# Keys of two batches and queries of the last rows turned by transposing transfers instead of TensorE, with a new order of work: a 4-batch attention and MLP kernel on one core

## Chip, cores and metric

One core of a Trainium2 chip runs the whole kernel. The time is device microseconds (us) of one execution. The kernel before took 652.37 us (median of 3 runs, 651.45 to 653.49).

## What is computed

Attention of 4 batches and 8 heads over 576 rows of 64 elements, with a bias that a small network makes from the distance of two rows, and then an MLP over the 2304 x 512 result:

```python
scores = scale * np.matmul(q, k.transpose(0, 1, 3, 2))
rel = (pos[:, None] - pos[None, :]).astype(np.float32)
psi_i = np.log1p(np.maximum(pos[:, None].astype(np.float32), 1.0))
x = (np.log1p(np.abs(rel)) / psi_i)[..., None]
bias = np.maximum(x @ w1 + b1, 0.0) @ w2          # hidden 32, one value per head
attn = softmax(scores + bias.transpose(2, 0, 1)[None])
h = attn_out @ w_in                               # 512 -> 2048
out = (h * (1.0 / (1.0 + np.exp(-1.702 * h)))) @ w_out
```

The weights come as 64-bit floats and are put together on VectorE.

## The kernel before

Every matmul that matters is made of fp16 halves: a value is scaled and rounded to fp16 (`hi`, on ScalarE or VectorE), and what is left over is rounded again (`lo`, always VectorE, helper `lo_part` at L735). A product takes three matmuls (hi hi, hi lo, lo hi).

The batches go in two pairs, (0, 1) and (2, 3). A pair has five chunks of query rows, c = 0 to 3 with 128 rows and c = 4 with the last 64. A *unit* is one batch, one chunk and one pair of heads (two pairs of heads for c = 4): 36 units a pair, 72 in all. A unit runs: scores on TensorE (L899) into the PSUM tile `sp`; bias added and row minimum taken on VectorE (L908); the exponential on ScalarE (L917); hi (L938 on ScalarE or L934 on VectorE) and lo (L735) of the weights into a `wide` tile; that tile turned so that the keys lie on partitions, and the matmuls with v (L1004). The first 8 units are turned on TensorE (L953, L958, copied out at L963 or L965) and multiplied at L980. The other 64 are turned by one transposing transfer each, issued by SP (L989), 18 blocks of 128 x 128 fp16. The halves of the result (`xT`) feed the MLP: L1211 (w_in), tanh and gate (L1219 to L1240), L1249 (w_out), eviction (L1255) and the store (L1265). The bias is made on TensorE from relu tiles (L621 on ScalarE, L623 on VectorE; products at L640), evicted (L643), stored to a scratch in DRAM (L659) and loaded per unit pair (L719).

Keys: per batch and half of the heads one tile (`load_k`, L797; e = 0, 1), 8 tiles in all. The key rows 512 to 575 of a pair of batches come apart (`load_kt`, L789). `trans_k` (L810) turns a tile on TensorE into `sp`: 8 fp32 transposes (L815) and two small matmuls for the last 64 keys (L816). ScalarE evicts the hi half (L830), VectorE the lo half (L835, shown as L735, 128 x 1152 from PSUM).

Queries: c = 1 to 3 of all batches and c = 0 of batches 2 and 3 are split in their own layout (L761, L763) and turned by a transposing transfer of 8 blocks on SP's queue (L766), 14 of them. The others, c = 0 of batches 0 and 1 and c = 4 of all four batches, are turned on TensorE (`trans_q`, L752 to L756).

The order is made while the program is built. Each piece of work is a task for one engine with its inputs, its estimated cost, the buffers it takes and gives back, and a priority. `Plan.order` (L58) plays the tasks through and, whenever an engine is free, gives it the ready task with the lowest number, if its buffers are free. The numbers come from the list `TURNS` (L230), one per task in the order in which the tasks are made; the strings `WHERE` (L220) say for each task that could run on either which engine it gets (A ScalarE, V VectorE, P GpSimd). The result is one fixed instruction order per engine and per DMA queue. All loads, all transposing transfers and all stores to the scratch are issued by SP, in one row. There are 18 `wide` buffers (128 x 1152 fp32) and 8 `narrow` ones (128 x 576); `LEAST` (L428) keeps at least so many of a kind free for each use.

A task with a `gate` starts only behind the scores of an earlier unit; for a key load that was 2 units before its first use (`K_FROM`, L446).

Of the kernel before, what the change touches and what calls it, by code (L numbers as in the profile page):

```python
# [1355 lines left out]
```

## Time and profile before

| what | value |
|---|---|
| median of 3 runs | 652.37 us (651.45 to 653.49) |
| the profiled execution | 654.06 us |
| its span | 652.3 us, 22886 instructions |
| TensorE matmul / weight load busy | 608.8 us (93%) / 432.6 us (66%) |
| VectorE / ScalarE / GpSimd busy | 509.2 (78%) / 398.6 (61%) / 74.6 us (11%) |
| transfers of SP's queue (q1) | 104.81 MB, 74.4% of the DMA engines' time |
| chain that ended last, by engine | PE 74%, DVE 14%, ACT 5%, issue 3%, DMA 2% |

A busy share is an average over stages; what bounds a stage is read from that stage's rows. TensorE's matmuls overlap, so its busy time stands for "had work", and idle time before an instruction says what it waited for. The span lies 1.8 us under the profiled execution's own time, and that execution 1.7 us over the median.

### The profile page before, as it was taken

To read this page: it belongs to the slowest core of one execution; us is meant where nothing else is said; L and a number is where in the kernel's file an instruction comes from. 1 tells how busy PE (TensorE), PEld (TensorE's weight loads), DVE (VectorE), ACT (ScalarE), POOL (GpSimd) and SP (SyncE) were. 2 spreads that over 40 slices of the span, in tenths; PEclk is the share of its full clock that TensorE was granted. 3 is DMA by queue.
4 is the path that set the end of the run, shared out by engine and by line. 5 is a ranking of instruction groups with operands and counts; after the bars stand their busy time and mean duration, and the time that the engine had idled before them with its cause. 6 is when DMAs were issued, how large, how long until landed. Compare 5 with 4: busy or idle time off the path is not lost.

```text
span 652.3 us, 22886 instructions
## 1 busy us (share of the span) xinstructions
PE 608.8 (93%) x9712; PEld 432.6 (66%) x9712; DVE 509.2 (78%) x1371; ACT 398.6 (61%) x870; POOL 74.6 (11%) x116
## 2 busy tenths in 40 slices
PE   5579877998899999999999999999999999999997
PEld 3236555675576667657677667677777777878775
DVE  7989997999997967783869999996895898423232
ACT  6988854988788745662657577665753655322222
POOL 3000000111110110011200010101112011001211
PEclk9969995999999999999999999999999999999999
DMA  9987863899969985989899999998986897500000
GB/s 273 310 285 229 219 215 111 170 236 232 214 232 205 166 164 121 193 173 216 199 202 197 191 188 212 218 173 134 208 196 110 150 158 124 95 34 4 2 35 18
DMA packets 227542, 111.08 MB, mean 170 GB/s; under 512 B 207088, under 2 KB 211824, under 8 KB 227440
## 3 DMA queue, kind: packets, MB, share of 16 engines
q1 hardware_dynamic: 224672, 104.81, 74.4%
q10 hardware_dynamic: 2768, 4.81, 2.2%
q8 instruction: 76, 1.25, 0.8%
q14 instruction: 26, 0.21, 0.1%
HBM read 52.85 MB, written 15.34 MB: 105 GB/s over the span
## 4 chain that ended last, share of the span: by engine, by line
PE 74%; DVE 14%; ACT 5%; issue 3%; DMA 2%; SPq 1%; ACTq 0%; DVEq 0%
PE hp L1211 26%; PE op L1249 25%; PE sp L899 8%; PE hp L1004 7%; PE sp L640 3%; DVE wide L908 3%; DVE wide L735 2%; PE op L640 2%; PE op L958 2%; ACT wide L621 2%; DVE w L735 1%; DVE narrow L1141 1%; DVE narrow L1145 1%; PE hp L980 1%; DMA scr<-narrow 1%
## 5 line engine op out<-in xcount | busy, mean ns | idle before, releaser
L1211 PE MATMUL hp<-xT,w 128*64 128x256 f16 (+1 forms) x3840 | 207.1, 262 | 1.6 <-DVE w L735 1.0
L1249 PE MATMUL op<-w,gT 128*64 128x512 f16 x1728 | 204.5, 380 | 3.5 <-ACT gT L1233 1.5
L1211 PEld LDWEIGHTS <-w 128*64 128x64 f16 x3840 | 189.6, 110 | 19.6 <-issue 7.7
L1249 PEld LDWEIGHTS <-gT 128*64 128x64 f16 x1728 | 96.4, 110 | 78.8 <-issue 6.7
L917 ACT ACTIVATE wide<-wide,sm 128x576 f32<-128x576 f32 x144 | 110.9, 770 | 47.9 <-DVE sm L908 43.1
L1240 POOL TENSOR_TENSOR gT<-th,gT 128x256 f16<-128x256 f32 (+1 forms) x95 | 69.6, 734 | 570.9 <-ACT gT L1233 336.1
L1219 ACT ACTIVATE th<-hp 128x256 f32<-128x256 f32 (+1 forms) x160 | 57.1, 357 | 117.0 <-PE hp L1211 88.3
L1225 DVE SCALAR_TENSOR_TENSOR th<-th,hp 128x256 f32<-128x256 f32 (+1 forms) x160 | 62.4, 391 | 77.6 <-ACT th L1219 76.3
L908 DVE CUSTOM_DVE_ANT_0 wide<-sp,wide 128x576 f32<-128x576 f32 x144 | 105.8, 751 | 6.9 <-PE sp L899 2.7
L735 DVE SCALAR_TENSOR_TENSOR wide<-wide,sm,wide 128x576 f16<-128x576 f32 x128 | 104.4, 826 | 6.6 <-ACT wide L938 6.2
L899 PE MATMUL sp<-wide,narrow 64*128 64x512 f16 (+1 forms) x960 | 67.1, 289 | 12.5 <-DVE sm L908 7.2
L938 ACT ACTIVATE wide<-wide,sm 128x576 f16<-128x576 f32 x83 | 62.4, 767 | 7.8 <-DVE sm L926 2.0
L1004 PEld LDWEIGHTS <-v 128*64 128x64 f16 x2160 | 57.9, 111 | 5.7 <-issue 2.6
L1004 PE MATMUL hp<-wide,v 128*64 128x128 f16 (+1 forms) x2160 | 60.5, 214 | 0.4 <-DMA wide<-wide 0.4
L899 PEld LDWEIGHTS <-narrow 64*128 64x128 f16 (+1 forms) x960 | 28.9, 98 | 46.5 <-issue 28.3
L621 ACT ACTIVATE wide<-tab,bp 128x576 f32<-128x576 f32 x81 | 59.2, 772 | 0.2 <-PE sp L640 0.2
L1233 ACT CAST gT<-th 128x256 f16<-128x256 f32 (+1 forms) x84 | 32.0, 380 | 27.8 <-DVE th L1225 17.0
L640 PE MATMUL op<-wide,pk 128*32 128x512 f32 (+1 forms) x208 | 23.3, 518 | 10.0 <-ACT narrow L643 3.5
L623 DVE TENSOR_SCALAR wide<-tab,bp 128x576 f32<-128x576 f32 x63 | 31.3, 527 | 0.0
L1240 DVE TENSOR_TENSOR gT<-th,gT 128x256 f16<-128x256 f32 (+1 forms) x65 | 25.3, 390 | 6.0 <-ACT gT L1233 5.2
L640 PE MATMUL sp<-wide,pk 128*32 128x512 f32 (+1 forms) x368 | 28.4, 443 | 1.0 <-DVE sm L908 0.9
L1235 DVE CAST gT<-th 128x256 f16<-128x256 f32 (+1 forms) x76 | 21.3, 280 | 9.4 <-PE op L1249 7.3
(72 smaller groups left out, 494.3 us busy)
## 6 DMA issues: line engine op xcount, KB each, us to landing
wide<-scr SPq DMA_DIRECT2D x32, 576.0 KB, 5.1
scr<-narrow SPq DMA_DIRECT2D x31, 288.0 KB, 3.7
wide<-in_moe_w_in_dram SPq DMA_DIRECT2D x16, 512.0 KB, 5.4
wide<-in_moe_w_out_dram SPq DMA_DIRECT2D x16, 512.0 KB, 4.8
wide<-in_k_dram SPq DMA_DIRECT2D x16, 256.0 KB, 5.1
narrow<-in_q_dram SPq DMA_DIRECT2D x16, 256.0 KB, 4.4
out_dram<-narrow ACTq DMA_DIRECT2D x16, 256.0 KB, 3.1
wide<-scr SPq DMA_DIRECT2D x8, 288.0 KB, 5.0
```

Source lines behind the costliest of these rows:

```text
L621: nc.scalar.activation(out=h, in_=tv, func=ACTF.Relu, bias=bp[:, pb:pb + 1])
L640: nc.tensor.matmul(to[32 * r:32 * r + 32], lhsT=w2b, rhs=rhs, start=True, stop=True)
L735: nc.vector.scalar_tensor_tensor(out=out, in0=in0, scalar=scale, in1=in1, op0=ALU.mult, op1=ALU.subtract)
L899: nc.tensor.matmul(pair[64 * e:64 * e + m, a, cs], lhsT=qt[r, x, hp + e, 0:m], rhs=kt[r, hp % 2 + e, y, cs], start=i == 0, stop=i == 2,)
L908: nc.vector.tensor_tensor_reduce(out=slot(("a32", u))[:, cs], in0=slot(("sp", u)).rearrange("p (h a) n -> p h (a n)", h=2)[:, a, 0:S], in1 ...
L917: nc.scalar.activation(out=t, in_=t, func=ACTF.Exp, scale=-1.0, bias=sm[:, a:a + 1], accum_out=sm[:, 2 + a:3 + a])
L938: nc.scalar.activation(out=hl_of(u)[:, 0, cs], in_=slot(("a32", u))[:, cs], func=ACTF.Identity, scale=r)
L1004: nc.tensor.matmul(o[64 * a:64 * a + 64, po], lhsT=vt[:, x, vc:vc + 64], rhs=t[:, 9 * y + k0, po], start=kb < 0 and i == 0, stop=kb == 3 a ...
L1211: nc.tensor.matmul(p[y0:y0 + FF, :n], lhsT=wi16[:, f // 4, cc, z, w0:w0 + FF], rhs=r, start=i == 0, stop=i == 11, skip_group_check=FF < 128,)
L1225: nc.vector.scalar_tensor_tensor(out=th, in0=th, scalar=1.0, in1=slot(("hp", j, f))[:, :n], op0=ALU.add, op1=ALU.mult)
L1240: (nc.vector if on("low", NF * j + f) == "V" else nc.gpsimd).tensor_tensor(out=gt[:, 1, :n], in0=th, in1=gt[:, 0, :n], op=ALU.subtract)
L1249: nc.tensor.matmul(o[y0:y0 + FF, i], lhsT=gt[:, z, 128 * i + y0:128 * i + y0 + FF], rhs=wo16[:, NF - 1 - f, y, :], start=f == 0 and n3 == ...
```

## The change

Four things change.

1. **Keys of batches 2 and 3.** The four key tiles are no longer turned on TensorE. They are split in their own layout (`k_split`: hi on ScalarE for batch 2 and VectorE for batch 3, lo on VectorE, 128 x 1024), and one transfer per tile turns both halves (`turn_k`, 16 blocks). The last 64 keys of both batches are split and turned once (`kt_split`, `turn_kt`, 8 blocks), into a `narrow` buffer that is held until the pair's last scores and for which `LEAST` now keeps one. The loads may start 9 units before the first use instead of 2.
2. **Queries of c = 4.** The two batches of a pair share one tile: two loads, one split, one transfer of 8 blocks. Four tasks on TensorE become two transfers.
3. **The last store.** The second of the last two stores is issued by SP instead of ScalarE.
4. **Order and engines.** All numbers in `TURNS` are new, and the strings too. Counts of tasks on (ScalarE, VectorE), before to after: relu (81, 63) to (86, 58); exp, the hi half of the weights, (95, 49) to (77, 67), of which units 42 to 59 hold 14; turn, the copies of the first 8 units, (16, 8) to (22, 2); x (26, 46) to (30, 42); gate hi (84, 76) to (76, 84); weight hi (22, 10) to (21, 11). Gate lo (GpSimd, VectorE) goes from (95, 65) to (102, 58).

```diff
+        'khi': 'AAAAAAVV',
...
-        'turn': 'AAAAVAVVAAAAVAAAVVAVAVAA',
+        'turn': 'AAAAAAAAAAAAVAAAAAVAAAAA',
...
-             "narrow": {"w": 1, "os": 2, "qT": 2, "q": 1, "kt": 1, "ob": 1, "dg": 1, "qs": 1}}
+             "narrow": {"w": 1, "os": 2, "qT": 2, "q": 1, "kt": 1, "ob": 1, "dg": 1, "qs": 1, "kTt": 1}}
...
-    TURNED_Q = {(b, c) for b in range(B) for c in range(4) if b > 1 or c > 0}
+    TURNED_Q = {(b, c) for b in range(B) for c in range(5) if b > 1 or c > 0}
+    TURNED_K, KT_FROM = {1}, 9
...
+    def q_key(b, c):
+        return (b, c) if c < 4 else (b // 2 * 2, c)
...
-        t = slot(("q32", b, c))[:n, 0:512].rearrange("p (h d) -> p h d", h=H)
-        nc.sync.dma_start(out=t, in_=q[b, :, 128 * c:128 * c + n, :].rearrange("h p d -> p h d"))
+        for i in range(1 if c < 4 else 2):
+            t = slot(("q32", b, c))[n * i:n * i + n, 0:512].rearrange("p (h d) -> p h d", h=H)
+            nc.sync.dma_start(out=t, in_=q[b + i, :, 128 * c:128 * c + n, :].rearrange("h p d -> p h d"))
...
+    def k_split(b, e, z):
+        t, d = slot(("k32", b, e))[:, 0:1024], slot(("ks", b, e)).bitcast(F16)
+        if z:
+            lo_part(d[:, 1024:2048], t, KS, d[:, 0:1024])
+        elif on("khi", 2 * b + e) == "A":
+            nc.scalar.activation(out=d[:, 0:1024], in_=t, func=ACTF.Copy, scale=KS)
+        else:
+            nc.vector.tensor_scalar(out=d[:, 0:1024], in0=t, scalar1=KS, scalar2=None, op0=ALU.mult)
+
+    def turn_k(b, e):
+        nc.sync.dma_start_transpose(
+            out=slot(("kT", b, e)).bitcast(F16)[:, 0:2048].rearrange("p (c n) -> p c n", c=16),
+            in_=slot(("ks", b, e)).bitcast(F16)[:, 0:2048],
+        )
...
+    def turn_kt(g):
+        nc.sync.dma_start_transpose(
+            out=slot(("kTt", g)).bitcast(F16)[:, 0:1024].rearrange("p (c n) -> p c n", c=8),
+            in_=slot(("kts", g)).bitcast(F16)[:, 0:1024],
+        )
+
+    def k_of(b, hp, y, cs):
+        if b // 2 not in TURNED_K:
+            return k_out(b, hp // 2)[:, hp % 2, y, cs]
+        if cs.start == 0:
+            return slot(("kT", b, hp // 2)).bitcast(F16)[:, 0:2048].rearrange("p (x u n) -> p x u n", x=2, u=2)[:, y, hp % 2]
+        t = slot(("kTt", b // 2)).bitcast(F16)[:, 0:1024].rearrange("p (x u n) -> p x u n", x=2, u=NP)
+        return t[:, y, hp, ST * (b % 2):ST * (b % 2) + ST]
+
+    def add_turned_k(b, e):
+        p, g = due(first["k", b, e]) - K_LEAD, b // 2
+        if g not in kt_task:
+            ld = add("SP", 700, lambda: load_kt(g), take=[("narrow", "kt", ("kt", g))],
+                     gate=first["k", b, e] - KT_FROM, prio=p - LOAD_LEAD, dma=1200, n_dma=2, hold=4000)
...
+            kt_task[g] = add("SP", 1300, lambda: turn_kt(g), [lo], take=[("narrow", "kTt", ("kTt", g))],
+                             give=[("kts", g)], prio=p, dma=1350, hold=2000)
+        ld = add("SP", 700, lambda: load_k(b, e), take=[("wide", "kv", ("k32", b, e))],
+                 gate=first["k", b, e] - KT_FROM, prio=p - LOAD_LEAD, dma=2300, n_dma=2, hold=4500)
+        hi = either("khi", 2 * b + e, lambda: k_split(b, e, 0), {"A": act(1024), "V": dve(1024, fast=True)}, [ld],
+                    take=[("wide", "ks", ("ks", b, e))], prio=p)
+        lo = add("DVE", dve(1024), lambda: k_split(b, e, 1), [hi], give=[("k32", b, e)], prio=p)
+        kT_task[b, e] = add("SP", 2400, lambda: turn_k(b, e), [lo, kt_task[g]], take=[("wide", "kT", ("kT", b, e))],
+                            give=[("ks", b, e)], prio=p, dma=2700, hold=2000)
...
-                nc.scalar.dma_start(out=out[t:t + hi - lo, :], in_=ob[lo - 128 * i:hi - 128 * i, :])
+                q_ = nc.sync if j == len(blocks) - 1 and off else nc.scalar
+                q_.dma_start(out=out[t:t + hi - lo, :], in_=ob[lo - 128 * i:hi - 128 * i, :])
```

Two places of the new order. TensorE, before, where the first key tile of batch 2 is turned (`wide_86` is the key tile, `narrow_102` the last 64 keys, `idn` the identity), between the MLP's matmuls:

```order
L1211 LDWEIGHTS w_63
L1211 MATMUL hp_123<-xT_114,w_63 64x256
L815 MATMUL sp<-idn,wide_86 128x128 x4
L816 MATMUL sp<-idn,narrow_102 128x64
L815 MATMUL sp<-idn,wide_86 128x128 x4
L816 MATMUL sp<-idn,narrow_102 128x64
L1249 LDWEIGHTS gT_119
L1249 MATMUL op<-w_63,gT_119 64x512
```

After, the same keys appear on TensorE only in the scores (L957 there), `wide_93` being the turned tile and `narrow_108` the turned last keys:

```order
L957 MATMUL sp<-wide_93,narrow_104 128x512
L957 LDWEIGHTS narrow_104
L957 MATMUL sp<-narrow_108,narrow_104 128x64
L957 LDWEIGHTS narrow_104
L957 MATMUL sp<-narrow_108,narrow_104 128x64
L957 LDWEIGHTS narrow_104
L957 MATMUL sp<-wide_93,narrow_104 128x512
```

The transposes and the small matmuls are gone from TensorE's row, for all four tiles; the scores keep their shapes.

SP's queue, before, around the key loads of the second pair (L989 an attention turn, L766 a query turn, L719 a bias load, L799 and L792 key loads; the L989 here is the 25th):

```order
L743 DMA narrow_105<-in_q_dram 128x8x64
L989 DMA_TRANSPOSE wide_88<-wide_94 128x18x128
L719 DMA wide_100<-scr_79 128x1152
L799 DMA wide_86<-in_k_dram 128x8x64 x2
L792 DMA narrow_102<-in_k_dram 64x8x64 x2
L766 DMA_TRANSPOSE narrow_105<-narrow_104 128x8x128
L799 DMA wide_91<-in_k_dram 128x8x64 x2
```

After, from the 22nd attention turn (L1047 there) to the 25th; L848 turns the last keys, L835 a key tile, L803 loads one, L723 a bias load, L770 a query turn:

```order
L1047 DMA_TRANSPOSE wide_100<-wide_88 128x18x128
L835 DMA_TRANSPOSE wide_93<-wide_89 128x16x128
L663 DMA scr_83<-narrow_106 128x576
L663 DMA scr_83<-narrow_107 128x576
L1047 DMA_TRANSPOSE wide_85<-wide_90 128x18x128
L1047 DMA_TRANSPOSE wide_91<-wide_96 128x18x128
L723 DMA wide_87<-scr_83 64x1152 x2
L723 DMA wide_99<-scr_83 64x1152 x2
L723 DMA wide_97<-scr_79 128x1152
L803 DMA wide_94<-in_k_dram 128x8x64 x2
L835 DMA_TRANSPOSE wide_88<-wide_101 128x16x128
L770 DMA_TRANSPOSE narrow_104<-narrow_102 128x8x128
```

The key loads moved ahead by several attention turns, and the key turns stand behind the 22nd, 24th, 25th and 27th attention turn, with the turn of the last keys ahead of the 22nd.

## Rows read from the trace of the kernel before

**Rows 1.** Stretches: us, busy us (x count) of PE, PEld, DVE, ACT, POOL; TensorE clock; DMA share; GB/s

```profile
0.00:120.00 120.00, 89.55 (x854) 56.02 (x854) 106.06 (x248) 88.18 (x166) 4.97 (x21) 0.89 0.76 229
120.00:180.00 60.00, 55.40 (x880) 37.14 (x878) 59.59 (x133) 50.15 (x103) 10.38 (x12) 1.00 1.01 223
...
220.00:335.00 115.00, 115.00 (x1836) 80.47 (x1834) 83.99 (x239) 64.68 (x142) 15.08 (x19) 1.00 0.88 180
335.00:450.00 115.00, 112.65 (x2100) 82.26 (x2096) 104.32 (x316) 74.69 (x180) 11.65 (x18) 1.00 1.02 192
450.00:565.00 115.00, 115.00 (x1978) 84.81 (x1974) 94.42 (x267) 65.24 (x151) 16.80 (x21) 1.00 0.83 152
565.00:652.00 87.00, 81.22 (x1486) 65.74 (x1482) 25.35 (x76) 21.46 (x61) 11.71 (x20) 1.00 0.08 20
sum 652.00, PE 608.82 PEld 432.62 DVE 509.25 ACT 398.56 POOL 74.62; mean PE 86.97 PEld 61.80 DVE 72.75 ACT 56.94 POOL 10.66
```

**Rows 2.** Waits of PE, 185 to 652 us: us in total, times, longest us

```profile
PE sp L899 <- DVE wide L735: 1.5, 2, 1.2
...
PE hp L1004 <- DMA wide<-wide: 0.4, 1, 0.4
```

**Rows 3.** Timeline of PE at the first key tile: start us, us, line, instruction

```profile
331.11 0.66 PE L815 MATMUL sp<-idn,wide 128*128 128x128 f32 x4
...
332.48 2.78 PE L1249 MATMUL op<-w,gT 128*64 128x512 f16 x24
```

**Rows 4.** Timeline of PE at a query tail of 64 rows

```profile
528.95 0.46 PE L756 MATMUL sp<-idn,narrow 64*128 64x64 f32 x4
529.34 1.50 PE L1211 MATMUL hp<-xT,w 128*64 128x256 f16 x24
```

**Rows 5.** Timeline of ACT and its queue at the end

```profile
647.87 0.60 ACT L1255 ACTIVATE narrow<-op 128x512 f32<-128x512 f32 x1 [1.55 <-PE op L1249]
648.50 1.14 ACTq L1265 DMA_DIRECT2D out_dram<-narrow  x2
```

**Rows 6.** DMA, 545 to 575 us: queue with share; transfers with count, median us to landing

```profile
q1 hardware_dynamic: 9344, 2.36, 49.7%
...
wide<-wide SPq DMA_TRANSPOSE x4, 5.1
```

**Rows 7.** Timeline of SP's queue: attention turns 21 and 22, and 25

```profile
279.53 5.91 SPq L989 DMA_TRANSPOSE wide<-wide  x2
...
317.36 3.44 SPq L989 DMA_TRANSPOSE wide<-wide  x1
```

**Rows 8.** DMA, 335 to 450 us, same columns

```profile
q1 hardware_dynamic: 60495, 20.99, 98.7%
...
wide<-wide SPq DMA_TRANSPOSE x19, 6.9
```

**Rows 9.** Chain of waits at 339.55 us, then PE's timeline at 344.33 us

```profile
339.55 4.74 DMA wide<-wide
...
344.33 1.14 PE L1004 MATMUL hp<-wide,v 128*64 128x64 f16 x60 [0.43 <-DMA wide<-wide]
```

**Rows 10.** Groups by line and form: xcount, busy us, mean ns, idle before us

```profile
L735 DVE SCALAR_TENSOR_TENSOR wide<-sp,wide 128x1152 f16<-128x1152 f32 x8 | 10.8, 1352 | 2.0 <-ACT wide L830 2.0
...
L735 DVE SCALAR_TENSOR_TENSOR narrow<-narrow,narrow 128x512 f16<-128x512 f32 x14 | 9.6, 686 | 0.1
...
L934 DVE TENSOR_SCALAR wide<-wide,sm 128x576 f16<-128x576 f32 x45 | 24.5, 547 | 0.1
...
L965 DVE COPY wide<-op 128x512 f32<-128x512 f32 x7 | 4.8, 689 | 4.5 <-PE op L958 4.2 <-ACT wide L963 0.3
...
L623 DVE TENSOR_SCALAR wide<-tab,bp 128x576 f32<-128x576 f32 x63 | 31.3, 527 | 0.0
```

**Rows 11.** Timeline of PE: scores of units 42 and 60

```profile
379.80 0.91 PE L899 MATMUL sp<-wide,narrow 64*128 64x512 f16 x12
...
477.72 0.91 PE L899 MATMUL sp<-wide,narrow 64*128 64x512 f16 x12
```

More of the change, by code (lines that the diff above doesn't have):

```diff
@@ L530, in due @@
         return U_AT[0] + U_AT[1] * u if u < 8 else U_AT[2] + U_AT[3] * (u - 8)
+    def q_key(b, c):
+        return (b, c) if c < 4 else (b // 2 * 2, c)
     first = {}
     for u, (b, c, hp) in enumerate(units):
-        for key in (("q", b, c), ("k", b, hp // 2)):
+        for key in (("q",) + q_key(b, c), ("k", b, hp // 2)):
             first.setdefault(key, u)
@@ L741, in load_q @@
         n = q_n(c)
[L742 to L743 removed]
+        for i in range(1 if c < 4 else 2):
+            t = slot(("q32", b, c))[n * i:n * i + n, 0:512].rearrange("p (h d) -> p h d", h=H)
+            nc.sync.dma_start(out=t, in_=q[b + i, :, 128 * c:128 * c + n, :].rearrange("h p d -> p h d"))
     def q_out(b, c):
[L746 removed]
+        return slot(("qT",) + q_key(b, c)).bitcast(F16)[:, 0:1024].rearrange("p (x n) -> p x n", x=2)
     def q_psum(b, c):
         t = slot(("qp", b, c))
[L750 removed]
+        return (t[:, 0] if plan.env["qp", b, c][0] == "s" else t)[:, 0:512]
     def trans_q(b, c):
[L753 to L754 removed]
+        t, p = slot(("q32", b, c))[:, 0:512], q_psum(b, c)
         for hp in range(NP):
[L756 removed]
+            nc.tensor.transpose(p[:, 128 * hp:128 * hp + 128], t[:, 128 * hp:128 * hp + 128], idn)
     def q_split(b, c, z):
@@ L771, in add_q @@
     def add_q(b, c):
-        n, p = q_n(c), due(first["q", b, c]) - Q_LEAD
-        ld = add("SP", 350, lambda: load_q(b, c), take=[("narrow", "q", ("q32", b, c))],
-                 gate=first["q", b, c] - Q_FROM, prio=p - LOAD_LEAD, dma=9 * n, hold=4000)
+        n, p = 128, due(first["q", b, c]) - Q_LEAD
+        ld = add("SP", 350 if c < 4 else 700, lambda: load_q(b, c), take=[("narrow", "q", ("q32", b, c))],
+                 gate=first["q", b, c] - Q_FROM, prio=p - LOAD_LEAD, dma=9 * n, hold=4000, n_dma=1 if c < 4 else 2)
         if (b, c) in TURNED_Q:
@@ new lines, in kt_split @@
+    def kt_split(g, z):
+        t, d = slot(("kt", g))[:, 0:512], slot(("kts", g)).bitcast(F16)
+        if z:
+            lo_part(d[:, 512:1024], t, KS, d[:, 0:512])
+        else:
+            nc.scalar.activation(out=d[:, 0:512], in_=t, func=ACTF.Copy, scale=KS)
+    def turn_kt(g):
[10 more added lines that the diff above has]
+        return t[:, y, hp, ST * (b % 2):ST * (b % 2) + ST]
@@ new lines, in add_turned_k @@
+    def add_turned_k(b, e):
[3 more added lines that the diff above has]
+                     gate=first["k", b, e] - KT_FROM, prio=p - LOAD_LEAD, dma=1200, n_dma=2, hold=4000)
+            hi = add("ACT", act(512), lambda: kt_split(g, 0), [ld], take=[("narrow", "qs", ("kts", g))], prio=p)
+            lo = add("DVE", dve(512), lambda: kt_split(g, 1), [hi], give=[("kt", g)], prio=p)
+            kt_task[g] = add("SP", 1300, lambda: turn_kt(g), [lo], take=[("narrow", "kTt", ("kTt", g))],
[7 more added lines that the diff above has]
+                            give=[("ks", b, e)], prio=p, dma=2700, hold=2000)
@@ L821, in add_k @@
     def add_k(b, e):
+        if b // 2 in TURNED_K:
+            return add_turned_k(b, e)
         p = due(first["k", b, e]) - K_LEAD
@@ L889, in scores @@
         m, ne = (128, 1) if c < 4 else (64, 2)
-        n = q_n(c)
         qt = q_out(b, c).rearrange("p x (u n) -> p x u n", u=NP)
-        kt = k_out(b, hp // 2)
+        q0 = 0 if c < 4 else ST * (b % 2)
         pair = slot(("sp", u)).rearrange("p (h a) n -> p h (a n)", h=2)
@@ L899, in scores @@
                         nc.tensor.matmul(
-                            pair[64 * e:64 * e + m, a, cs], lhsT=qt[r, x, hp + e, 0:m], rhs=kt[r, hp % 2 + e, y, cs],
+                            pair[64 * e:64 * e + m, a, cs], lhsT=qt[r, x, hp + e, q0:q0 + m], rhs=k_of(b, hp + e, y, cs)[r],
                             start=i == 0, stop=i == 2,
@@ L1052 @@
             wb, wc, whp = units[w]
-            for kind, key, fn in (("k", (wb, whp // 2), add_k), ("q", (wb, wc), add_q), ("v", (wb, whp // 2), add_v)):
+            for kind, key, fn in (("k", (wb, whp // 2), add_k), ("q", q_key(wb, wc), add_q), ("v", (wb, whp // 2), add_v)):
                 if (kind, key) not in made:
@@ L1059 @@
         e2 = 1 if c < 4 else 2
-        st = s_task[u] = add("PE", 735, lambda u=u: scores(u), [qT_task[b, c], kT_task[b, hp // 2]],
+        st = s_task[u] = add("PE", 735, lambda u=u: scores(u), [qT_task[q_key(b, c)], kT_task[b, hp // 2]],
                              after=([s_task[u - 1]] if u else []) + [bias_pe[c]], mode=1,
@@ L1101 @@
             x_task[u] = add("DVE", 200, lambda u=u: x_split(u, 1), [go], give=[("ot", u)], prio=p - X_FIRST)
-            plan.extra(s_task[u], [("kT", b, hp // 2), ("qT", b, c)])
+            plan.extra(s_task[u], [("kT", b, hp // 2), ("qT",) + q_key(b, c)] + [("kTt", b // 2)] * (b // 2 in TURNED_K))
             continue
```

21 lines of the change are left out of this document (8 added, 13 removed), and 385 rows, old and new, of the table TURNS.

## The prediction

> **What bounds the kernel now.** I read the busy time by stretches first, because the whole-span shares mix two different regimes [rows 1]. In the first 180 us TensorE is idle for 30.5 us (120 less 89.55) and then 4.6 us (60 less 55.40), and its mean granted clock is 0.89 of full in the first 120 us: it waits for others. From 120 to 180 us VectorE is busy for 59.59 of 60 us, so that stretch is VectorE's, with the DMA at 1.01 beside it. From 220 us on the picture turns over. TensorE is busy in all of 220 to 335 us and all of 450 to 565 us, and in 112.65 of the 115 us between. At full clock, with no idle time, it sets the end: an instruction taken off it there moves everything behind it forward.
>
> The waits of TensorE behind 185 us say how near the other limits are [rows 2]. The largest is for VectorE, 1.5 us in all; a wait for a turned tile is there once, 0.4 us. So the order fits, but the stretch 335 to 450 us is tight three times over: TensorE full, VectorE 104.32 of 115 us, DMA share 1.02 [rows 1].
>
> **The change part by part.** *Keys off TensorE.* The first key tile of batch 2 starts at 331.11 us and the next work at 332.48 us: 1.37 us [rows 3]. All four tiles show this distance and lie between here and 373 us, so 4 x 1.37 = 5.5 us, where TensorE hardly waits. The scores keep their matmuls, so nothing comes back on TensorE.
>
> *Queries of 64 rows off TensorE.* One takes 529.34 less 528.95 = 0.39 us [rows 4], four of them 1.6 us, two at each pair's end, in the stretches without idle time. Again on the path.
>
> *Last store.* ScalarE ends the last eviction and issues two stores in 1.14 us [rows 5], 0.57 us each. With SP issuing the second at the same time, 0.55 us goes, bounds 0 and 0.6. Nothing else is queued on SP then; all its turns are long done.
>
> *DMA time added.* Where four attention turns run almost alone, the queue is busy for 49.7% of 30 us = 14.9 us, so 3.7 us for 18 blocks [rows 6], 0.21 us a block. A key turn (16 blocks) is then 3.3 us and a turn of 8 blocks 1.65 us. Four and three of them (last keys, two query tails): 18.2 us of DMA time, for 7.1 us of TensorE. The changed order puts two key turns, the last keys and one query tail near the 22nd to 24th attention turns, and two key turns behind the 25th and 27th. In the trace before, the 21st is issued at 279.53 us and the 25th at 317.36 us [rows 7]; the transfer of 339.55 us is the 27th by count. So 9.9 us falls ahead of about 335 us and 6.6 us behind; the second query tail comes near 530 us, where the DMA has 17% free [rows 1], and is hidden. From 220 to 335 us the DMA has 12% free, 14 us [rows 1]; from 335 to 450 us SP's queue alone takes 98.7%, which leaves 1.5 us, and a turn needs 6.9 us to landing against 5.1 us when alone [rows 8]. If half of the 14 us can be used (a turn can start only when its data is there), 16.5 less 7 = 9.5 us makes later turns late. How much of it reaches TensorE? Turn and matmul stand close: a turn issued at 339.55 us landed after 4.74 us and TensorE had waited 0.43 us for it [rows 9]. But the loads of keys now go ahead of the crowd, and MLP work is left over: behind 565 us TensorE still works for 81.22 us [rows 1], nearly all of it MLP. Bounds 0 and 16.5 us; I take 2 us, near the lower end, because a queue just as full cost TensorE only 0.4 us in all [rows 2].
>
> Which unit should turn is a point on which the Trainium skill has a rule, page "VectorE: DVE Perf Modes", section "Rules for kernel authors": a 128 x 128 transpose belongs on TensorE when PSUM may be its target, and on the DMA crossbar only otherwise; the section "The three transpose paths" has 390 ns against 1309 ns a block. By those figures the 88 blocks moved are an estimated 115 us of DMA, and the sum would be about 746 us if only the free 14 us hid any. The trace does not agree in size (0.21 us a block) and agrees in direction: more DMA time than TensorE time.
>
> *Splits.* VectorE loses four lo halves of 1152 from PSUM at 1352 ns [rows 10] and gains four of 1024 from SBUF. No row shows that form; 512 takes 686 ns [rows 10], so two of them, 1.37 us, are the upper end, and 1352 x 1024/1152 = 1.20 us the lower; I take 1.24. With two hi halves of 1024 (0.92 us each, from 527 ns for 576 columns [rows 10]) and one lo of 512 it is 7.5 against 5.4 us: 2.1 us more. ScalarE gets less of this work.
>
> *Engines re-dealt, second half.* Units 42 to 59 give 14 hi halves to VectorE, at 547 ns 7.7 us [rows 10]. These units run from 379.80 to 477.72 us [rows 11], where VectorE has 9.3% of 70 us and 17.9% of 28 us free [rows 1], 11.5 us, for the 9.8 us of both. If it fits, nothing; if VectorE is late, scores wait for its row minimum, as they do today. Bounds 0 and 9.8 us; I take 1 us, nearest the present 1.5 us of such waits.
>
> *Engines re-dealt, first 180 us.* VectorE loses five copies of 512 (689 ns) and one small one (some 0.3 us), and three relus at 527 ns [rows 10]: 5.3 us where it is full. ScalarE takes them; it was busy for 50.15 of 60 us, so it has room on average. Against it stands one `narrow` buffer of eight that is kept for the turned last keys from the start: bias evictions, weight merges and query tiles share those. No row prices that; the nearest is the whole idle time of TensorE in this stretch, 35 us, of which a seventh would be 5 us. Bounds 5.3 gained and 5 lost; I take 1 us gained, near the middle since nothing favours an end.
>
> *The rest of the new order.* TensorE's tasks are the same; where they stand costs only through waits, which the terms above hold.
>
> **Sum.** 5.5 + 1.6 + 0.55 + 1 less 2 less 1 = 5.65 us gained. The profiled execution took 654.06 us (span 652.3 and 1.8 around it), so 648.4; that execution stood 1.7 us over the median, so against the median of 652.37 it is **646.7 us**.
>
> **Rivals.** *The DMA becomes the bound from 300 to 450 us* (slower). For it: 98.7% of the queue taken, SP issues in one row, so a key turn that waits for VectorE's lo half also holds the attention turns behind it. Against it: the loads go 7 units earlier and the free 14 us lie just ahead. It decides once more than 9.6 us of the added 16.5 us (the 7.65 us saved and the 2 us of a measurable loss) reach TensorE. With 9.5 us the time is 652.37 less 7.65 plus 9.5 = 654.2 us, with all 16.5 us 661.2; I put it at 657. The skill's rule above speaks for this rival.
>
> *The first 180 us get longer* (no change). With the `narrow` buffer costing its 5 us and none of the VectorE relief passed on, the gain falls by 6: 646.7 + 6 = 652.7 us. For it: that stretch waits on others all the time. Against it: of the query tails only one tile a pair now holds such a buffer, where two did.
>
> *Everything fits* (faster still). No wait for DMA or VectorE appears and the first stretch passes on its 5.3 us: 652.37 less 7.65 less 5.3 = 639.4 us. For it: VectorE full from 120 to 180 us. Against it: work moved to ScalarE lies on the same chains.
>
> *The change does not do what it says*: closed, the changed order has none of the transposes of batches 2 and 3 on TensorE.
>
> **How the numbers follow.** Forecast 0.50, DMA bound 0.17, first stretch longer 0.16, everything fits 0.17. A measurement of this kernel can tell 0.3%, 2 us, so faster means under 650.4 and slower over 654.3: faster 0.50 + 0.17 = 0.67, no change 0.16, slower 0.17. The forecast's own range, with the DMA and VectorE terms together between 0 and 7 us, is 643.7 to 650.7. The range has to take in 652.7 and reaches to 639 and to 656.5, so that it leaves out about half of the DMA rival and little else.
>
> **What would show it.** Right: no matmul of the transposing lines behind 300 us; TensorE busy in all of 220 to 335 us and in over 110 of the next 115 us; waits of TensorE for turned tiles of 2 us or so. The forecast is wrong if TensorE waits for DMA by over 8 us between 300 and 450 us, if SP's queue waits long at a key turn, or if TensorE's idle time in the first 180 us moves by more than 3 us from 35.

## The result, and the profile after

The changed kernel took 644.94 us (median of 6 runs, 642.35 to 645.61), beside it the kernel before 652.18 us (6 runs, 650.47 to 653.77): ratio 0.9879 [0.9853, 0.9905], so 1.2% faster; the medians lie 7.2 us apart. In later runs it took 644.17 us (0.9880 [0.9861, 0.9899]). The predicted 646.7 us lies 1.8 us off, and the range held it. The two profiled executions lie further apart than the medians (spans 652.3 and 640.5 us), so a difference of the two traces is up to 4.6 us too large.

The stretches of the changed kernel, columns as in [rows 1]:

```profile
0.00:120.00 120.00, 90.10 (x888) 54.77 (x890) 107.46 (x251) 92.82 (x177) 6.68 (x23) 0.90 0.80 237
120.00:180.00 60.00, 57.32 (x930) 39.93 (x928) 59.03 (x135) 50.92 (x105) 13.06 (x14) 1.00 1.04 236
...
220.00:335.00 115.00, 114.32 (x1928) 82.32 (x1926) 88.38 (x238) 64.90 (x146) 17.50 (x21) 1.00 0.97 191
335.00:450.00 115.00, 110.48 (x2043) 81.00 (x2038) 102.29 (x310) 64.61 (x166) 14.14 (x23) 1.00 0.97 192
450.00:565.00 115.00, 115.00 (x2002) 84.11 (x2000) 96.55 (x273) 59.88 (x140) 16.25 (x22) 1.00 0.84 155
565.00:640.00 75.00, 71.29 (x1288) 55.66 (x1282) 23.82 (x71) 18.64 (x53) 9.80 (x18) 1.00 0.06 21
sum 640.00, PE 598.36 PEld 423.24 DVE 516.21 ACT 385.06 POOL 82.16; mean PE 85.48 PEld 60.46 DVE 73.74 ACT 55.01 POOL 11.74
```

TensorE is busy for 598.36 us where it was 608.82. Its idle time in the first 180 us is 32.6 us (29.90 and 2.68) against 35.1. From 335 to 450 us, where the keys went, it is idle for 4.5 us against 2.35: a part of what was freed there became waiting (3.9 us of idle time in the second execution, `after_again`). ScalarE has 10 us less to do in that stretch. The DMA share from 220 to 335 us rose from 0.88 to 0.97, as the key turns would have it.

TensorE's waits from 185 us to the end (us in total, times, longest):

```profile
PE hp L1269 <- DVE th L1283: 3.7, 5, 1.6
PE hp L1062 <- DVE th L1283: 0.7, 2, 0.4
PE hp L1269 <- DVE xT L739: 0.6, 1, 0.6
```

No wait for a transfer is among them (before: 0.4 us [rows 2]). All 5.0 us are for VectorE: in 3.7 of them the first MLP matmul (L1269) waits until VectorE has read the `hp` bank before last. The longest lies at 347 us, right behind the scores of a turned key tile:

```profile
345.58 0.19 PE L957 MATMUL sp<-narrow,narrow 64*128 64x64 f16 x2
347.34 2.81 PE L1269 MATMUL hp<-xT,w 128*64 128x256 f16 x48 [1.57 <-DVE th L1283]
```

The kernel before waited for VectorE 1.9 us behind 185 us (1.5 [rows 2] and 0.4 for a row minimum).

SP's queue issues the four key turns (L835) ahead of the place where the keys stood on TensorE (331 us on [rows 3]):

```profile
282.71 2.90 SPq L835 DMA_TRANSPOSE wide<-wide  x1
300.35 7.53 SPq L835 DMA_TRANSPOSE wide<-wide  x1
316.44 3.57 SPq L835 DMA_TRANSPOSE wide<-wide  x1
326.61 2.06 SPq L835 DMA_TRANSPOSE wide<-wide  x1
```

The new splits, by form (xcount, busy us, mean ns), to be held against [rows 10]:

```profile
L739 DVE SCALAR_TENSOR_TENSOR wide<-wide,wide 128x1024 f16<-128x1024 f32 x4 | 5.3, 1330 | 0.0
L832 DVE TENSOR_SCALAR wide<-wide 128x1024 f16<-128x1024 f32 x2 | 1.4, 690 | 0.0
```

And ScalarE with its queue, then SP's, at the end [rows 5]:

```profile
636.33 0.60 ACT L1313 ACTIVATE narrow<-op 128x512 f32<-128x512 f32 x1 [1.86 <-PE op L1307]
636.95 0.52 ACTq L1324 DMA_DIRECT2D out_dram<-narrow  x1
```

```profile
636.95 0.51 SPq L1324 DMA_DIRECT2D out_dram<-narrow  x1
```

### The profile page after: what moved, and what is told of

It reads as the page before. It is cut to its first block, busy times and chain, and to the rows that moved or that the text cites. A ratio compares the mean times of both kernels' runs of the same rounds, so it can differ in the third digit from the quotient of the medians.

```text
span 640.5 us, 22783 instructions
## 1 busy us (share of the span) xinstructions
PE 598.4 (93%) x9648; PEld 423.2 (66%) x9648; DVE 516.2 (81%) x1381; ACT 385.1 (60%) x851; POOL 82.2 (13%) x123
## 4 chain that ended last, share of the span: by engine, by line
PE 70%; DVE 17%; ACT 6%; DMA 4%; issue 2%; ACTq 0%; SPq 0%; DVEq 0%
PE op L1307 25%; PE hp L1269 24%; PE hp L1062 7%; PE sp L957 7%; DVE wide L966 3%; DVE wide L739 3%; PE sp L644 3%; ACT wide L625 2%; DMA wide<-scr 2%; PE op L644 2%; PE op L1016 1%; DVE th L1283 1%; DVE v L739 1%; DVE narrow L1199 1%; DVE narrow L1203 1%
## 5 line engine op out<-in xcount | busy, mean ns | idle before, releaser
L1269 PE MATMUL hp<-xT,w 128*64 128x256 f16 (+1 forms) x3840 | 207.3, 262 | 7.6 <-DVE th L1283 4.3
L1269 PEld LDWEIGHTS <-w 128*64 128x64 f16 x3840 | 189.7, 110 | 26.7 <-issue 16.9
L1298 POOL TENSOR_TENSOR gT<-th,gT 128x256 f16<-128x256 f32 (+1 forms) x102 | 77.1, 757 | 551.0 <-ACT gT L1291 278.5
L1283 DVE SCALAR_TENSOR_TENSOR th<-th,hp 128x256 f32<-128x256 f32 (+1 forms) x160 | 62.1, 390 | 64.4 <-ACT th L1277 63.6
L966 DVE CUSTOM_DVE_ANT_0 wide<-sp,wide 128x576 f32<-128x576 f32 x144 | 105.7, 750 | 6.1 <-PE sp L957 4.2
L739 DVE SCALAR_TENSOR_TENSOR wide<-wide,sm,wide 128x576 f16<-128x576 f32 x128 | 106.2, 843 | 3.0 <-ACT wide L996 2.7
L957 PE MATMUL sp<-wide,narrow 64*128 64x512 f16 (+2 forms) x720 | 67.3, 326 | 6.0 <-DVE sm L966 4.0
L625 ACT ACTIVATE wide<-tab,bp 128x576 f32<-128x576 f32 x86 | 62.8, 774 | 0.0
L957 PEld LDWEIGHTS <-narrow 64*128 64x128 f16 (+1 forms) x960 | 28.4, 98 | 41.2 <-issue 23.5
L996 ACT ACTIVATE wide<-wide,sm 128x576 f16<-128x576 f32 x65 | 48.8, 768 | 7.8 <-DVE sm L984 5.3
L1291 ACT CAST gT<-th 128x256 f16<-128x256 f32 (+1 forms) x76 | 29.1, 383 | 27.2 <-PE op L1307 13.6
L992 DVE TENSOR_SCALAR wide<-wide,sm 128x576 f16<-128x576 f32 x63 | 34.5, 556 | 0.2
L1298 DVE TENSOR_TENSOR gT<-th,gT 128x256 f16<-128x256 f32 (+1 forms) x58 | 23.1, 397 | 8.7 <-ACT gT L1291 7.6
L982 DVE TENSOR_SCALAR sm<-sm 128x1 f32<-128x1 f32 (+1 forms) x128 | 19.8, 154 | 12.7 <-ACT wide L975 12.3
L627 DVE TENSOR_SCALAR wide<-tab,bp 128x576 f32<-128x576 f32 x58 | 29.1, 530 | 0.8 <-PE sp L644 0.8
```

The source lines that it names most:

```text
L625: nc.scalar.activation(out=h, in_=tv, func=ACTF.Relu, bias=bp[:, pb:pb + 1])
L739: nc.vector.scalar_tensor_tensor(out=out, in0=in0, scalar=scale, in1=in1, op0=ALU.mult, op1=ALU.subtract)
L957: nc.tensor.matmul(pair[64 * e:64 * e + m, a, cs], lhsT=qt[r, x, hp + e, q0:q0 + m], rhs=k_of(b, hp + e, y, cs)[r], start=i == 0, stop=i == 2,
L966: nc.vector.tensor_tensor_reduce(out=slot(("a32", u))[:, cs], in0=slot(("sp", u)).rearrange("p (h a) n -> p h (a n)", h=2)[:, a, 0:S], in1 ...
L1269: nc.tensor.matmul(p[y0:y0 + FF, :n], lhsT=wi16[:, f // 4, cc, z, w0:w0 + FF], rhs=r, start=i == 0, stop=i == 11, skip_group_check=FF < 128,)
L1283: nc.vector.scalar_tensor_tensor(out=th, in0=th, scalar=1.0, in1=slot(("hp", j, f))[:, :n], op0=ALU.add, op1=ALU.mult)
```

## The experiments

The theory: the gain is the TensorE work that went, 7.1 us, and the DMA hides what took its place. The rivals: the new order and the new split between ScalarE and VectorE bring it; or the DMA has nothing left and decides. A change of one part moves the planner's whole order, so in all kernels below except the changed one the order is written out, task by task, and so is the buffer that each tile gets:

```diff
-        for fn in plan.order():
+        for fn in plan.replay(ORDER, BUFFERS):
             fn()
```

With the changed kernel's own two lists every engine's instructions are those of the changed kernel. Ratios are to the kernel before on the same chip; "against the changed kernel" is the difference to 0.9880, times 652.4 us.

### TensorE's work put back: where the keys stood, and later

```diff
+        if u in KEYS_AT:
+            for z in range(2):
+                for w in range(4):
+                    nc.tensor.transpose(pair[:, z, 128 * w:128 * w + 128], idn, idn)
+                nc.tensor.matmul(pair[:, z, SM:S], lhsT=idn, rhs=idn[:, 0:ST], start=True, stop=True)
+        if u in TAILS_AT:
+            for w in range(4):
+                nc.tensor.transpose(pair[:, 0, ST * w:ST * w + ST], idn[:ST, :], idn[:ST, :ST])
...
+    KEYS_AT, TAILS_AT = (36, 37, 40, 41), (30, 32, 66, 68)
```

`pe_back`. 

> The changed kernel, its order, engines and transfers untouched, with as much TensorE work put back as the change took off: ahead of the scores of the four units that first read a turned key tile, eight 128x128 transposes and two tail matmuls of the identity, and ahead of four units of the last rows four 64-row transposes, all into the score tile that the scores then overwrite. Nothing of the result changes. Theory 1 (the gain is the TensorE work that went, 4 x 1.37 + 4 x 0.39 = 7.1 us, in stretches without idle time): 5 to 7 us slower than the changed kernel, so within 2 us of the kernel before. Theory 2 (the gain is the new order and the new split between ScalarE and VectorE; TensorE had room): at most 2 us slower than the changed kernel, still 5 us faster than before.

Measured: 647.66 us, 0.9915 [0.9888, 0.9943]: 2.3 us over the changed kernel, uncertain by 2.2, and 5.5 us (3.7 to 7.3) under the kernel before. TensorE's timeline in `pe_back` at the first key tile put back:

```profile
321.21 0.66 PE L958 MATMUL sp<-idn 128*128 128x128 f32 x4
...
322.59 0.39 PE L968 MATMUL sp<-wide,narrow 64*128 64x512 f16 x2
...
325.98 0.30 PE L1280 MATMUL hp<-xT,w 128*64 128x256 f16 x2 [1.05 <-DVE th L1294]
```

From 321.21 to 322.59 us it takes 1.38 us, as [rows 3] has it, and 3.4 us later TensorE waits for VectorE all the same. So the work is there. The profiled spans (645.6 and 640.5 us) do not say what it costs, because the changed kernel's profiled execution lies 2.6 us under its median and that of `pe_back` 0.2 us. A stretch of the two traces says more. From the scores of unit 34 to those of unit 48, with all four key tiles between them, first in the changed kernel and then in `pe_back`:

```profile
309.19 0.93 PE L957 MATMUL sp<-wide,narrow 64*64 64x512 f16 x24
401.15 0.39 PE L957 MATMUL sp<-wide,narrow 64*128 64x512 f16 x2
```

```profile
309.77 0.94 PE L968 MATMUL sp<-wide,narrow 64*64 64x512 f16 x24
405.88 0.39 PE L968 MATMUL sp<-wide,narrow 64*128 64x512 f16 x2
```

That is 91.96 us (91.35 in `after_again`) against 96.11: 4.2 to 4.8 us for 5.5 us of work. From the scores of unit 24 to the end of TensorE's last matmul it is 408.6 and 407.9 us against 413.8: 5.2 to 5.9 us for all 7.1. Ahead of unit 24, where nothing was put back, the traces that share the changed kernel's first stretch differ among themselves by 4 us (the scores of unit 24 start between 226.46 and 230.42 us).

So by the medians the work costs a third of its length, by the traces most of it, and nothing here decides between the two. The medians fit the second theory: at most 2 us over the changed kernel is within the uncertainty, and 5 us under the kernel before came out with all of TensorE's work put back. The first theory's "within 2 us of the kernel before" did not. Its 5 to 7 us over the changed kernel is what the traces show.

`pe_late`: the same, with `KEYS_AT = (60, 61, 64, 65)`. 

> As pe_back (7.1 us of TensorE work put back into the changed kernel), but the four key tiles' share of 5.5 us stands ahead of the scores of units 60, 61, 64 and 65, between 470 and 510 us, where TensorE of the changed kernel has no idle time, and not ahead of units 36 to 41, where it waits for VectorE 5.0 us in all. If those waits took up the work in pe_back (it cost 2.5 to 3 us there): 6 to 8 us slower than the changed kernel, 651 to 653 us. If TensorE's work costs less than its time everywhere: 647 to 649 us again.

Measured: 650.60 us, 0.9955 [0.9931, 0.9978]: 4.9 us over the changed kernel, uncertain by 1.9, where 6 to 8 were expected. Its trace also holds a wait of TensorE of 2.0 us, up to 346.70 us, for which the profile shows no cause, far ahead of the key tiles' share of the work put back. From the scores of unit 56 to those of unit 65, with the four key tiles between, first in the changed kernel and then in `pe_late`:

```profile
454.79 0.39 PE L957 MATMUL sp<-wide,narrow 64*128 64x512 f16 x2
506.27 0.39 PE L957 MATMUL sp<-wide,narrow 64*128 64x512 f16 x2
```

```profile
455.56 0.39 PE L968 MATMUL sp<-wide,narrow 64*128 64x512 f16 x2
512.52 0.39 PE L968 MATMUL sp<-wide,narrow 64*128 64x512 f16 x2
```

That is 51.48 us (the same in `after_again`) against 56.96: 5.5 us for 5.5 us of work. So in the stretch without idle time TensorE's work costs its whole length, and where the keys stood 0.7 to 1.3 us less (by the medians 2.6 us less for all of it, uncertain by 2.3). There it takes the place of waits for VectorE: TensorE's idle time from 220 to 450 us is 3.7 us in `pe_back`, 5.2 and 4.5 us in the two executions of the changed kernel.

### Is it the amount of VectorE's work?

`exp_old`, letters 84 to 119 of the string, which are units 42 to 59:

```diff
-VAVAAVVAVVVVVVVVVAVVAVVVAVAVVAVVAVVV
+AAAAAAVVVAAAVAAVAAVVAAAAAAVAAAAVAVVV
```

> The changed kernel in its own order, with one string undone: the hi halves of the exponentials of units 42 to 59 are on the engines of the kernel before (14 fewer on VectorE, 14 more on ScalarE, some 0.56 us each on VectorE, 7.8 us). The first runs left this open: 7.1 us of TensorE work put back cost only some 2.5 us, as if VectorE, for which TensorE waits 5.0 us behind 185 us, set the pace where the keys went. Theory V (VectorE sets the pace from 335 to 450 us): 2 to 4 us faster than the changed kernel, waits of TensorE for VectorE under 2.5 us. Forecast (VectorE's added work costs 1 us): at most 1 us either way. Rival (ScalarE is late instead): 1 to 3 us slower, with waits of TensorE for ScalarE.

Measured: 645.55 us, 0.9889 [0.9868, 0.9910], 0.6 us over the changed kernel, uncertain by 1.9. VectorE's busy time from 335 to 450 us fell from 102.29 to 96.85 us, and TensorE waited for it no less, 6.0 us in all, most of it here:

```profile
PE hp L1064 <- DVE th L1285: 2.2, 2, 1.4
PE hp L1271 <- DVE th L1285: 2.0, 4, 0.7
```

So theory V falls (2 to 4 us faster lies outside the interval): the sum of VectorE's work is not what TensorE waits for. VectorE's timeline of the changed kernel at the longest wait, 347 us, shows what is, at that one place:

```profile
345.82 0.76 DVE L966 CUSTOM_DVE_ANT_0 wide<-sp,wide 128x576 f32<-128x576 f32 x1 [0.38 <-PE sp L957]
...
346.50 0.42 DVE L1283 SCALAR_TENSOR_TENSOR th<-th,hp 128x256 f32<-128x256 f32 x1
```

The gate's multiplication (L1283), for which TensorE waits, stands in VectorE's queue behind a row minimum (L966) that had itself waited for TensorE's scores. By this reading a matmul less on TensorE would not shorten such a turn; that was not tested, and whether the other waits are of this kind was not taken apart.

### The parts without the new order

`parts_old`: the changed kernel's code, with the strings and the order of the kernel before.

```diff
+        'khi': 'AAAAAAVV',
...
-    TURNS = [
+    ORDER = [
```

> The kernel before with the change's parts alone: keys of the second pair and queries of the last 64 rows split in natural layout and turned by transfers, last store by two queues, but everything else in the old order and on the old engines (the new steps stand at the units at which the changed kernel has them). Theory 1: TensorE loses the same 7.1 us in stretches without idle time, and gives back 2 us or so for DMA waits: 645 to 648 us. Theory 2 (the order and the split bring the gain): 650 to 654 us. Rival (the old order leaves the DMA no room for 18 us more behind 300 us): 652 to 657 us, with waits of TensorE for turned tiles of over 4 us in all.

Measured: 674.87 us, 1.0335 [1.0308, 1.0362]. This was my own doing in large part: a new step had been given the first buffer on the free list, and a buffer counted as free once its last reader stood earlier in the program, done or not. VectorE waited 9.7 us for a turn still reading such a buffer, in one case. `first_old` and `turn_twice` below had the same fault. So these three say nothing on the change.

`parts_old2`: the buffer that has been free longest, and better places for the new steps. 

> As parts_old (the kernel before with the change's parts alone, old order, old engines), but each step gets the buffer that has been free longest, and the 28 steps of the turned keys and queries stand where they fit best between the old ones; in parts_old row minima of the scores waited up to 9.7 us for a turn that still read the buffer they were given. Theory 1 (the TensorE work that went is the gain, in any order): 645 to 647 us. Theory 2 (the parts need the new order): 649 to 653 us. Rival (the DMA sets the pace in the old order): over 654 us, with waits on SP's bias loads.

Measured: 657.82 us (12 runs), 1.0061 [1.0037, 1.0085]: slower than the kernel before by 4.0 us and than the changed kernel by 11.8 (uncertain by 2.0), though TensorE has the same 7.1 us less to do. Its two largest groups of waits, 185 us to the end:

```profile
PE hp L1271 <- DVE th L1285: 7.6, 3, 3.8
PE hp L1064 <- DMA wide<-wide: 3.2, 3, 2.0
```

Waits for turned tiles are there now, and behind the longest wait for VectorE stands a transfer too. VectorE's timeline shows it: a row minimum of the scores (L968) waits 5.10 us for its bias, and the gate's multiplication (L1285) stands behind it.

```profile
313.86 0.76 DVE L968 CUSTOM_DVE_ANT_0 wide<-sp,wide 128x576 f32<-128x576 f32 x1 [5.10 <-DMA wide<-scr]
...
317.24 0.41 DVE L1285 SCALAR_TENSOR_TENSOR th<-th,hp 128x256 f32<-128x256 f32 x1
```

SP's queue shows when the bias loads (L725) go out:

```profile
305.76 1.27 SPq L772 DMA_TRANSPOSE narrow<-narrow  x1
307.12 2.65 SPq L725 DMA_DIRECT2D wide<-scr  x2
309.83 1.31 SPq L850 DMA_TRANSPOSE narrow<-narrow  x1
311.18 1.87 SPq L725 DMA_DIRECT2D wide<-scr  x3
```

There are five, and the row minimum waits for the first two, which fill the two halves of one tile; the view of these two names who waited for them:

```profile
L725 SPq DMA_DIRECT2D wide<-scr x2: 592/1301/2010, 307.1 to 309.2; - x2
...
  DVE wide L968: 5.1, 1
```

They stand ahead of the turn of the last keys (L850), so it is not this turn that made them late. In the kernel before the five were issued together, 2.7 us earlier:

```profile
304.42 3.14 SPq L719 DMA_DIRECT2D wide<-scr  x5
```

New in the row ahead of them are a query turn (issued at 276.43 us, in 2.20 us), the loads of the last keys (278.68, 1.31) and those of a key tile (290.32, 1.36). The two attention turns and the two scratch stores behind these took 7.40 and 2.63 us to issue, where the kernel before had 6.55 and 0.99. The first two key turns then stand in front of the 25th attention turn, which is issued at 323.23 us instead of 317.36 [rows 7].

So the DMA rival is real in the old order, by way of SP's row: what the change adds has to stand somewhere in a queue that works in order, and there it stood in front of loads that were just in time. How much of the delay is the row and how much the DMA time added was not separated. The new order issues its five bias loads at 295.49 us. How far 11.8 us overstate the worth of the new order is open: I placed the new steps, and a better place in the old order may exist.

### How much room the DMA has left

`turn_half`:

```diff
-            out=slot(("kT", b, e)).bitcast(F16)[:, 0:2048].rearrange("p (c n) -> p c n", c=16),
-            in_=slot(("ks", b, e)).bitcast(F16)[:, 0:2048],
+            out=slot(("kT", b, e)).bitcast(F16)[:, 0:1024].rearrange("p (c n) -> p c n", c=8),
+            in_=slot(("ks", b, e)).bitcast(F16)[:, 0:1024],
...
-            return slot(("kT", b, hp // 2)).bitcast(F16)[:, 0:2048].rearrange("p (x u n) -> p x u n", x=2, u=2)[:, y, hp % 2]
+            return slot(("kT", b, hp // 2)).bitcast(F16)[:, 0:2048].rearrange("p (x u n) -> p x u n", x=2, u=2)[:, 0, hp % 2]
```

> The changed kernel with the four key turns cut to the 8 blocks of the hi halves; the scores of the second pair read the hi half in place of the lo half, so that part of their sum is left out of the computation, and nothing else moves. It takes 6.6 us of DMA time (4 x 1.65) out of the stretch from 280 to 335 us. Forecast (the turns are hidden): within 1 us of the changed kernel. Rival (the DMA sets the pace there): 3 to 6 us faster.

Measured: 642.98 us, 0.9858 [0.9817, 0.9899]: 1.4 us under the changed kernel, uncertain by 2.9. SP's share of the DMA from 220 to 335 us fell from 93.3% to 88.4%:

```profile
q1 hardware_dynamic: 57649, 19.92, 88.4%
```

That is 5.6 us of 115 (6.6 were estimated). The interval reaches to 4.3 us faster, into the rival's 3 to 6; the trace does not. From the scores of unit 24 to the end of the last matmul it is 409.3 us here and 408.6 and 407.9 us in the changed kernel. So this half of the key turns is hidden.

`turn_twice`, and the same for the last keys' turn:

```diff
+        nc.sync.dma_start_transpose(
+            out=slot(("k32", b, e)).bitcast(F16)[:, 0:2048].rearrange("p (c n) -> p c n", c=16),
+            in_=slot(("ks", b, e)).bitcast(F16)[:, 0:2048],
+        )
...
-                            give=[("ks", b, e)], prio=p, dma=2700, hold=2000)
+                            give=[("ks", b, e), ("k32", b, e)], prio=p, dma=2700, hold=2000)
```

> The changed kernel with the four key turns and the turn of the last keys issued twice, the second time into the tile the keys were loaded to, which is given up only then; the order is the same. It adds 14.9 us of DMA time (4 x 3.3 + 1.65) between 275 and 335 us. The profile of the changed kernel shows 10 us of free DMA time from 220 to 450 us (3% and 3% of 115 us by the share, 6.7% and 5.7% by the queue, which is 14 us). Forecast's mechanism (hidden while the DMA has room): 0 to 5 us slower. Rival (the cover is used up): 8 to 15 us slower, with waits of TensorE for turned tiles or of VectorE for bias loads.

Measured: 673.13 us, 1.0311 [1.0283, 1.0339], with the buffer fault told above. (The free DMA time by the share, for which the expectation has 10 us, is 6.9 us: 3% and 3% of 115.) `turn_twice2` is without the fault. 

> As turn_twice (key turns and last keys' turn issued twice, 14.9 us of DMA time more from 275 to 335 us), with every step in the buffer that is free longest; in turn_twice a hi half at 279 us waited 4.4 us for a turn that still read its buffer, before any second key turn was issued. Cover left (hidden in the 10 to 14 us of free DMA time): 0 to 3 us slower than the changed kernel. Cover used up: 8 to 15 us slower, with row minima waiting for bias loads that stand behind the turns.

Measured: 659.26 us, 1.0085 [1.0059, 1.0112]: 13.4 us over the changed kernel (uncertain by 2.1) for 14.9 us of DMA time. Its output differs from that of the changed kernel, for a cause that is open, so it is read for its time alone. TensorE's first long wait and the next ones:

```profile
283.00 3.67 PE L646 MATMUL sp<-wide,pk 128*32 128x512 f32 x32 [3.85 <-DVE sm L976]
...
332.61 2.77 PE L1279 MATMUL hp<-xT,w 128*64 128x256 f16 x24 [4.58 <-DVE th L1293]
...
348.98 0.39 PE L967 MATMUL sp<-wide,narrow 64*128 64x512 f16 x2 [1.67 <-DMA narrow<-narrow]
```

The 3.85 us at 283 us are still the buffer's: the tile of the loaded keys, held longer, leaves one fewer. The rest, some 9.5 us, is paid for 14.9. Of these waits only the 1.67 us name a transfer; what lies behind the 4.58 us for VectorE was not followed. From the scores of unit 24 on the trace has 15.5 to 16.2 us more than the changed kernel, so with the buffer's wait taken off about 12. So the change uses up most of the room: half of its key turns less gains nothing that can be measured, as much again costs two thirds of its length or more.

### The first stretch alone

`first_new` (the old kernel with the changed kernel's order and strings up to the scores of unit 24) and `first_old` (the reverse) join the two orders there. Of `first_new`, one of its strings and the order:

```diff
-        'turn': 'AAAAVAVVAAAAVAAAVVAVAVAA',
+        'turn': 'AAAAAAAAAAAAVAAAAAVAAAAA',
...
-    TURNS = [
+    ORDER = [
```

> The kernel before in all its steps, with the changed kernel's order and engines up to the scores of unit 24 (about 230 us), and its own order and engines behind that; no step is removed or added. Theory 1: the first stretch is worth 0 to 2.5 us (TensorE's idle time in the first 180 us fell from 35.1 to 32.6 us): 650 to 652 us. Theory 2 (the new order gains): unit 24 began 5.5 us earlier in the changed kernel's profiled execution, and all of it stays: 646 to 648 us.

Measured: 651.37 us (12 runs), 0.9981 [0.9960, 1.0001]: 1.2 us under the kernel before, uncertain by 1.3. The second half here has waits that the kernel before lacks (2.6 us once for a turned tile), so the first stretch may be worth more.

> The changed kernel, with the order and engines of the kernel before up to the scores of unit 24 and its own behind that. Theory 1: 1 to 2.5 us slower than the changed kernel, 646 to 647.5 us. Theory 2 (the order of the first stretch brings most of the gain): 649 to 651 us.

Measured: 658.75 us, 1.0088 [1.0062, 1.0114], with the buffer fault. `first_old2` is without it. 

> As first_old (the changed kernel with the order and engines of the kernel before up to the scores of unit 24), with every step in the buffer that is free longest; in first_old row minima waited 2.2 and 2.6 us for such a buffer. Forecast (the new order of the first stretch is worth 1 us): 645 to 647 us. Rival (it is worth about 5 us, the 5.5 us by which unit 24 starts earlier): 648 to 651 us.

Measured: 646.76 us, 0.9890 [0.9858, 0.9923]: 0.7 us over the changed kernel, uncertain by 2.5. The first 230 us of the new order are worth 1 us or so, from both sides, and neither figure is clear of nothing.

### The changed kernel again

> The changed kernel as it is, on the chip of the next three, so that they are compared with it directly. Both theories: 643 to 646 us.

Measured: 644.17 us (643.08 to 646.31), 0.9880 [0.9861, 0.9899]. TensorE's waits behind 185 us were 4.2 us in all, again only for VectorE. No kernel that does all the work was measurably faster.

## Why the prediction was right, and where only its sum was

Most of the signs it named came out: no transposing matmul behind 300 us, TensorE busy for 114.32 of 115 and then 110.48 of 115 us, 2.5 us less idle time in the first 180 us, and SP's queue held at a key turn for 3.2 us at most. One did not: of the 2 us or so of waits for turned tiles there were none. Term by term it is another picture.

- **Keys and query tails off TensorE, 7.1 us.** The matmuls went and came back nowhere. But the term was sized too high: by the medians the same work put back costs 2.3 us (uncertain by 2.2) at its old place and 4.9 us (uncertain by 1.9) later, by the traces 5.2 to 5.9 us at its old place. The step that was too simple is "where TensorE hardly waits": ahead of 450 us its waits rose from 2.3 us to 5.0 (4.2 in `after_again`), and work put back there fills some of them.
- **The rest of the new order, nothing.** This is the step that was wrong. `pe_back` has all of TensorE's work back and is still 5.5 us (3.7 to 7.3) faster than the kernel before; with the parts alone in the old order the kernel is 4.0 us slower. I had priced where steps stand through the DMA term alone, 2 us, and not asked what the old order would do with them. The errors have opposite signs, and that the sum came out within 1.8 us is luck.
- **Added DMA time, 2 us.** In the new order it costs nothing that shows: no wait for a transfer, and nothing gained in the trace of `turn_half`. The prediction put two key turns behind 335 us, by the old kernel's times; all four are issued by 326.61 us. The room is nearly gone, as the rival said. Its mechanism, a queue that holds what stands behind, appeared in `parts_old2` and not in the changed kernel. By the figures of the Trainium skill (page "VectorE: DVE Perf Modes", section "The three transpose paths") the sum would have been an estimated 746 us; no run here shows anything near that, and where the key turns and the last keys' turn were issued twice, in `turn_twice2`, it cost some 10 us. The rule of the Trainium skill in the section "Rules for kernel authors" of that page, TensorE where PSUM may be the target and the DMA crossbar otherwise, agrees in direction with `parts_old2` alone.
- **VectorE, 1 us.** The lo half of 1024 columns takes 1330 ns (1.24 us taken, 1.37 us the bound), the hi half 690 (0.92 taken). The 14 hi halves cost nothing measurable: undone, the time moves by 0.6 us, uncertain by 1.9. Waits for VectorE grew all the same, from 1.9 to 5.0 us. They do not follow its load (`exp_old`), and the longest comes from its place in VectorE's queue.
- **First 180 us, 1 us.** Idle time fell by 2.5 us, `first_new` gives 1.2 us (uncertain by 1.3), `first_old2` 0.7 (uncertain by 2.5).
- **Last store, 0.55 us.** From the end of the last eviction to the end of the span it is 3.6 us (640.5 less 636.93) against 3.8. That is 0.2 us: the two stores are issued side by side, but the span ends only behind their landing.

By the medians, then, 5.5 us come with the new order, the splits and the transfers taken together, about 1 us of it in the first 230 us, and 2.3 us with TensorE's work; by the traces TensorE's work is worth more than that. What in the order behind 230 us brings its part was not taken apart further.

## What to carry to other kernels

When work moves from the bounding engine to a queue that works in order, ask what stands behind it in that queue: the same parts came with 7 us gained in one order and with 4 us lost in another. Test a saved piece of work by putting it back where it stood and where the engine never waits; the difference says how much of it only filled a wait. Read it over a stretch around the place, beside the medians, because two whole executions differ by more than the piece. If the kernel stays faster with the work back, the gain has another cause. A transfer that is hidden tells nothing of the next one: double it before you build on the room.

## What the runs showed of the hardware

A wait on TensorE can cost more than its length. In `parts_old2` TensorE works until 313.87 us and then waits for 3.84 us; the stretches after it (columns as in [rows 1]):

```profile
315.00:316.00 1.00, 0.00 (x0) 0.00 (x0) 0.67 (x5) 1.00 (x4) 0.00 (x0) 1.00 1.05 221
...
317.00:317.70 0.70, 0.00 (x0) 0.00 (x0) 0.66 (x2) 0.70 (x2) 0.00 (x0) 0.50 1.06 421
317.70:319.00 1.30, 1.29 (x14) 1.29 (x15) 1.11 (x4) 0.39 (x3) 0.63 (x1) 0.50 1.07 286
...
320.00:321.00 1.00, 1.00 (x26) 0.42 (x25) 0.41 (x2) 0.54 (x3) 0.74 (x1) 0.81 1.16 382
```

The granted clock falls from 1.00 (2.4 GHz) to 0.50 (1.2 GHz) at the end of the wait, is still 0.50 while the work has begun again, and 0.81 from 320 to 321 us. The 24 MLP matmuls that follow the wait take 2.77 us, against 1.50 us [rows 4] at full clock. So this wait cost at least 5.1 us instead of 3.84. In the changed kernel, whose longest wait is 1.57 us, the clock from 340 to 350 us stays at 1.00:

```profile
340.00:350.00 10.00, 8.43 (x226) 6.94 (x220) 7.12 (x21) 5.11 (x12) 0.00 (x0) 1.00 1.08 281
```

The length of one wait alone does not tell the two apart. In `pe_late` the clock is at 0.50 behind the wait of 1.97 us that ends at 346.70 us, and in `turn_twice2`, from 361 to 364 us, behind one of 1.49 us that ends at 360.81 us, shorter than the 1.57 us above. The row of `pe_late`:

```profile
347.00:350.00 3.00, 3.00 (x32) 2.20 (x30) 2.16 (x5) 0.40 (x1) 0.00 (x0) 0.50 0.91 203
```

From 220 to 450 us the mean clock of `parts_old2` is 0.98, which is up to 4.6 us (1% and 3% of 115 us) beside its 11.9 us of waits.
